# One hand-written order of 2293 steps, replaced by another order of the same steps

## The chip, the cores and the metric

The kernel runs on one core of one Trainium2 chip. The metric is the device time of one execution in microseconds (us), as the median of several runs. The core has five engines that each run their own instructions in order: TensorE (PE, matrix products; its weight loads are listed apart as PEld), VectorE (DVE), ScalarE (ACT), GpSimd (POOL) and SyncE (SP). SP here does nothing but issue DMAs. They meet only through semaphores: an instruction that needs another engine's result waits for it, and everything behind it on its own engine waits too.

## The reference

The kernel computes attention over pooled keys and values, and behind it a layer norm with a feed-forward block:

```python
def _attn_ref(q, k, v):                      # 8 batches, 8 heads, 576 rows, 64 wide
    k_p = k.reshape(B, H, S // 8, 8, D).mean(axis=3)
    v_p = v.reshape(B, H, S // 8, 8, D).mean(axis=3)
    scores = scale * np.matmul(q, k_p.transpose(0, 1, 3, 2))
    scores = scores - np.max(scores, axis=-1, keepdims=True)
    attn = np.exp(scores)
    attn = attn / (np.sum(attn, axis=-1, keepdims=True) + 1e-09)
    return np.matmul(attn, v_p)

def _moe_ref(x, g_ln, w_ch1, w_ch2):         # x: 8 x 576 x 512, w_ch1: 512 x 2048
    mu = np.mean(x, axis=-1, keepdims=True)
    var = np.mean((x - mu) ** 2, axis=-1, keepdims=True)
    xn = (x - mu) / np.sqrt(var + 1e-06) * g_ln
    ch = np.maximum(xn @ w_ch1, 0.0) @ w_ch2
    return x + ch
```

The attention's output, transposed to rows of 512, is the `x` of the second function. All is float32.

## The kernel before

The 4608 rows are 36 tiles of 128, and 9 chunks of four tiles (512 rows). Every step below is a piece of a Python generator: a call such as `A.30` (scores and softmax of tile 30) runs in several pieces, cut where the generator yields, and each piece issues a few instructions, mostly on one engine.

Attention of a tile `t`: `Q`/`A` load q (`load_q`, line 440), compute the scores on PE (line 447), on DVE the row maximum (457) and the difference `e` (460), on ACT the exponential (469) and casts to two float16 halves (480, 483), on POOL part of the second half (488, 491), and transpose through a DMA on SP (499). `B.t` multiplies with the values (534, or 536 and 537), forms the sums on DVE (544 to 554) and ACT (562) in one of 8 buffers `x`, runs the layer norm's 11 small DVE instructions (567 to 571), makes `z` on ACT (576) and from it float16 forms, which PE transposes (587) or a DMA does (613, 636). Scores and values share a pair of PSUM banks.

Keys and values of the batches are loaded and pooled: `HK` (`half_k`, line 1100) and `HV` (`half_v`, line 1103) issue one load per head or pair into a single buffer `kr` or `vr` (lines 395, 399) and fold it on DVE (1065, 1074). The last piece of `HV` runs `split_v` (line 408): a cast, and four small DMAs on ACT's own queue (lines 422, 423).

The feed-forward block keeps float32 accuracy with float16 high and low parts of weights and `z`. `R`, `C`, `M1`, `M2`, `S`, `T`, `F`, `N` load, convert, scale and split the two weight matrices, `S` with the DVE operation of line 309. Chunks 0 and 1 run it straight: `I` (`ffn_in`, matmuls of line 999), `O`/`P` (`ffn_out`, line 1034, with the sum on DVE, 1045, and the store, 1050). For chunks 2 to 8 the first product is done as seven half-size products of sums, as in Strassen's scheme: `U.c.g.n` is product `n` of group `g` of chunk `c` (`slot`, line 791; matmuls of line 726), each followed by a step that takes its bank out, on ACT (797, 801, 804) or DVE (799, 834, 851), and makes the forms in `ring` (769 to 784, 836, 845). `E.c.p.n` is the same for the second product (`slot2`, line 932; matmuls of line 943; DVE 956, 965, 975, 981, ACT 963, 967). Its weight forms come from DRAM by `D` (`w2_stream`, load of line 924) and `J`. `OUT.t` stores a finished tile from its `x` buffer (`put_out`, line 985).

What sets the order of all this is the string `START` alone (lines 56 to 200): under `tc.manual_schedule()` a loop takes its tokens from left to right, and each runs the next piece of its generator. So the order of tokens is the order of instructions on each engine and on each DMA queue (SP's, and ACT's for lines 422 and 423), and the order in which buffers and PSUM banks are taken in turn. No planner runs; there are no due times.

Of the kernel before, what the change touches and what calls it, by code (L numbers as in the profile page):

```python
# [66 lines left out]
C.2.4 I.0.0.0 A.5 I.0.0.1 I.0.0.0 C.2.2.1.1 A.5 I.0.0.0 I.0.1.0 I.0.0.1 I.0.1.0 C.2.4 I.0.0.1 S.1.4 I.0.1.0 A.5
I.0.0.0 C.2.2.1.1 R.2.7 I.0.0.0 I.0.0.1 HK.2.1 S.1.5 R.2.1 HK.2.0 A.6 I.0.1.0 S.1.5 I.0.0.1 HK.2.1 I.0.1.1
C.2.5.0.1 A.7 I.0.1.0 I.0.0.1 S.1.6 A.6 I.0.0.1 C.2.5.0.1 I.0.1.1 A.6 I.0.0.1 I.0.0.1 I.0.0.1 A.6 I.0.1.1 S.1.6
I.0.1.1 C.2.5.0.1 A.6 A.7 I.0.0.1 I.0.1.1 C.2.7 I.0.0.1 A.8 B.4 I.0.1.1 S.1.7 X.0 C.2.7 HV.2.0 I.0.1.1  # L70
C.2.5.0.1 A.6 C.2.7 HV.2.0 C.2.1.1 C.2.1.1 A.7 S.1.7 I.0.3 I.0.1.1 C.2.7 I.0.1.1 C.2.1.1 I.0.1.1 I.0.3 I.0.3
# [5 lines left out]
T.0.0.1 B.7 B.5 O.0.0 O.0.0 S.2.6 B.6 Y.2 B.6 HV.3.1 B.5 HK.2.1 T.0.0.1 HV.3.1 B.6 HK.3.0 HK.2.1 T.0.0.1 B.5
A.9 A.10 O.0.0 O.0.0 B.6 A.9 S.2.6 B.6 A.9 N.1.2 S.2.7 HV.3.1 B.6 A.9 HK.3.0 A.10 HV.3.1 O.0.0 S.2.7 A.11 A.9
HK.3.0 HK.3.0 A.10 N.1.3 O.0.1 T.1.0.1 A.9 A.10 HV.3.1 A.10 HV.3.1 T.0.1.1 HK.3.0 I.1.1 O.0.1 HK.3.1 O.0.1 B.8
T.1.0.1 I.1.3 T.0.1.1 I.1.1 B.8 HK.3.0 I.1.1 I.1.1 I.1.3 T.1.0.1 HV.3.1 I.1.3 HV.2.1 B.8 A.10 T.1.0.1 I.1.3  # L80
I.1.1 T.1.0.1 A.10 I.1.1 B.8 I.1.1 HV.2.1 T.1.0.1 HK.3.1 HV.2.1 I.1.3 HK.3.1 HK.3.1 I.1.3 I.1.3 I.1.1 B.8 I.1.1
# [1166 lines left out]
```

## Time and profile before

| what | value |
|---|---|
| median of 3 runs | 838.24 us (837.81 to 839.14) |
| profiled execution | 839.05 us |
| its span, first to last instruction | 837.3 us |
| instructions | 16786 |
| busy: PE, DVE, ACT, POOL | 799.1, 650.9, 462.5, 294.6 us |
| mean granted TensorE clock | 0.980 of full speed |
| DMA moved | 128.49 MB, mean 153 GB/s |

The page and the views come from one execution. The time outside its span, 1.75 us, is start and end of the launch. PE's busy time includes waits inside pipelined matmuls, so a share of 95% is not 95% of peak. In a view of waits, a row names the engine and operation that stood still and the instruction whose end released it. In a timeline, the text in brackets says how long the engine was idle before a row and what it had waited for; an engine with "q" behind its name is the engine's own issuing of DMAs.

### The profile page before, as it was taken

What the parts mean: (1) busy time and instruction counts of PE and PEld (TensorE: products, weight loads), DVE (VectorE), ACT (ScalarE), POOL (GpSimd) and SP (SyncE); (2) the same over time, 40 slices, a digit from 0 to 9 for tenths busy, and PEclk for the clock granted to TensorE, in tenths of its full rate; (3) what the DMA queues carried; (4) which work ended last, traced back from release to release, by engine and by line L of the source; (5) the groups of instructions that cost most, each with busy time, mean ns of one, the idle gap of its engine ahead of it and who ended that gap; (6) DMA issues with size and microseconds to landing.
All of it is one profiled execution on the core that took longest, in us unless ns stands there. A gap on an engine that the chain in (4) does not pass through costs nothing.

```text
span 837.3 us, 16786 instructions
## 1 busy us (share of the span) xinstructions
PE 799.1 (95%) x6554; PEld 624.8 (75%) x6554; DVE 650.9 (78%) x1371; ACT 462.5 (55%) x890; POOL 294.6 (35%) x260
## 2 busy tenths in 40 slices
...
GB/s 307 387 213 179 253 274 245 160 108 134 93 136 97 103 97 207 178 198 114 127 177 161 169 155 185 102 159 132 205 81 101 117 166 72 112 72 108 102 51 101
DMA packets 204639, 128.49 MB, mean 153 GB/s; under 512 B 123040, under 2 KB 181392, under 8 KB 201488
## 3 DMA queue, kind: packets, MB, share of 16 engines
...
## 4 chain that ended last, share of the span: by engine, by line
PE 63%; DVE 25%; ACT 5%; issue 3%; DMA 3%; POOL 0%; DVEq 0%; SPq 0%; ACTq 0%; POOLq 0%
PE ps_f L726 21%; PE ps_f L943 17%; PE ps_f L1034 12%; PE ps_f L999 7%; PE ps L447 2%; DVE a L516 2%; DVE x L956 2%; DVE w L309 2%; DVE y L519 2%; DVE st L567 2%; DMA pt<-phl 2%; DVE ring L784 1%; PE ps_f L1136 1%; DVE vp L1074 1%; DVE w L347 1%
## 5 line engine op out<-in xcount | busy, mean ns | idle before, releaser
L943 PE MATMUL ps_f<-w,ring 128*128 128x256 f16 x2016 | 229.0, 273 | 2.4 <-DVE ring L771 0.7
L943 PEld LDWEIGHTS <-ring 128*128 128x128 f16 x2016 | 196.3, 98 | 27.5 <-issue 2.0
L726 PE MATMUL ps_f<-zz,w 128*128 128x256 f16 x1344 | 159.6, 272 | 6.0 <-ACT v L804 5.5
L726 PEld LDWEIGHTS <-w 128*128 128x128 f16 x1344 | 130.7, 98 | 23.4 <-issue 7.2
L1034 PE MATMUL ps_f<-w,ring 128*128 128x512 f16 x576 | 127.6, 379 | 0.0
L726 PE MATMUL ps_f<-zz,raw 128*128 128x256 f16 x1008 | 120.8, 273 | 4.3 <-DVE v L834 1.8
L726 PEld LDWEIGHTS <-raw 128*128 128x128 f16 x1008 | 97.8, 98 | 18.3 <-issue 5.2
L778 POOL TENSOR_TENSOR ring<-v,ring 128x512 f16<-128x512 f32 x48 | 59.8, 1248 | 134.1 <-ACT ring L775 131.2
L1034 PEld LDWEIGHTS <-ring 128*128 128x128 f16 x576 | 56.0, 98 | 64.0 <-issue 0.2
L999 PE MATMUL ps_f<-zz,w 128*128 128x512 f16 (+1 forms) x480 | 86.9, 341 | 0.6 <-DVE ring L1013 0.5
L488 POOL TENSOR_TENSOR phl<-e,phl 128x512 f16<-128x512 f32 x31 | 37.7, 1217 | 106.8 <-ACT phl L480 85.5
L999 PEld LDWEIGHTS <-w 128*128 128x128 f16 x480 | 47.4, 100 | 36.6 <-issue 0.7
L634 POOL TENSOR_TENSOR hl<-z,hl 128x512 f16<-128x512 f32 x28 | 34.2, 1241 | 58.1 <-ACT hl L632 47.7
L447 PE MATMUL ps<-kblk,q 128*128 128x144 f32 (+1 forms) x320 | 46.3, 310 | 5.8 <-DVE e L460 3.9
L576 ACT ACTIVATE z<-x,nb,y 128x512 f32<-128x512 f32 x36 | 29.3, 815 | 40.5 <-DVE nb L571 40.5
L447 PEld LDWEIGHTS ps<-kblk,q 128*128 128x128 f32 (+1 forms) x320 | 40.5, 193 | 9.2 <-issue 5.5
L562 ACT ACTIVATE x<-ps,rs 128x64 f32<-128x64 f32 x144 | 33.0, 318 | 19.7 <-DVE x L554 15.2
L778 POOL TENSOR_TENSOR ring<-ring 128x512 f16<-128x512 f32 x24 | 29.5, 1228 | 39.8 <-ACT ring L775 36.9
L480 ACT CAST phl<-e 128x1024 f16<-128x1024 f32 x31 | 32.4, 1045 | 19.9 <-DMA pt<-phl 19.1
L469 ACT ACTIVATE e<-e 128x576 f32<-128x576 f32 x36 | 24.6, 683 | 26.0 <-DVE e L460 19.0
L1074 DVE TENSOR_REDUCE vp<-vr 72x64 f32<-72x512 f32 x48 | 32.3, 673 | 6.5 <-DMA vr<-in_v_dram 6.5
L457 DVE TENSOR_REDUCE mx<-ps 128x8 f32<-128x576 f32 x36 | 26.9, 749 | 12.0 <-PE ps L447 10.6
...
## 6 DMA issues: line engine op xcount, KB each, us to landing
...
```

What stands on the lines that cost most here:

```text
L447: nc.tensor.matmul(ps[r, p // 2, p % 2 * 2 * KV : (p % 2 + 1) * 2 * KV], lhsT=q[:, p, r], rhs=kblk[b % NKB][:, p, :], start=True, stop=True,)
L480: nc.scalar.copy(out=ph[:, :, :, 0:KA], in_=e[:, :, 0:KA].unsqueeze(1).broadcast_to([P, 2, H, KA]))
L488: nc.gpsimd.tensor_tensor(out=ph[:, 0, :, KA:P], in0=e[:, :, 0:KA], in1=ph[:, 0, :, 0:KA], op=ALU.subtract)
L562: nc.scalar.activation(out=xh[:, 4 + i, :], in_=px[:, 1, i, 0:D], func=AF.Copy, scale=rs[:, 4 + i : 5 + i])
L576: nc.scalar.activation(out=z, in_=x, func=AF.Identity, scale=y, bias=nb)
L634: nc.gpsimd.tensor_tensor(out=hl[:, 1, r], in0=part, in1=hl[:, 0, r], op=ALU.subtract)
L726: nc.tensor.matmul(ps[:, j], lhsT=w_form(wb, int(m == 2), k)[:, fs], rhs=z_form(za, int(m == 1), k), start=(first and i == 0 and j == 0), ...
L778: eng.tensor_tensor(out=lo, in0=src, in1=hi, op=ALU.subtract)
L943: nc.tensor.matmul(ps[:, i * HC : (i + 1) * HC], lhsT=h[:, hp, f, i * P : (i + 1) * P], rhs=w[:, f // FPB, wp, f % FPB], start=(first and ...
L999: nc.tensor.matmul(ps, lhsT=w[:, part, fs], rhs=zT[:, kz, cols], start=(n == 0), stop=(n == 3 * NKT - 1),)
L1034: nc.tensor.matmul(ps, lhsT=h[:, part, i, cols], rhs=w[:, wp, j], start=(n == 0), stop=(n == 3 * NFT // 2 - 1),)
L1074: nc.vector.tensor_reduce(out=vp[b][:, h, 0:D], in_=vraw.pop((b, h)), axis=AX.X, op=ALU.add,)
```

## The change

The diff has one hunk, and it is the text of `START`. Both lists hold the same 2293 tokens, each as often. 213 of them stand at the same place in the list; the mean move is 5.4 places, the longest 120. Functions, tiles, buffer counts and instructions stay. In the cut below, each group shows lines of the old list (with `-`) and the lines of the new one that stand nearest to the same steps.

```diff
...
-B.3 S.1.3 C.2.3 B.2 M1.1 A.4 C.2.3 A.4 I.0.0.0 B.3 C.2.0.1.1 C.2.0.1.1 C.2.3 B.3 C.2.4 C.2.0.1.1 I.0.1.0
-I.0.0.0 B.3 C.2.0.1.1 M1.1 B.2 I.0.1.0 R.2.2 C.2.3 A.4 A.5 B.2 R.2.5 A.4 I.0.0.0 I.0.1.0 A.6 I.0.0.0 M1.1 B.3
+S.1.3 A.4 C.2.3 S.1.3 C.2.3 I.0.1.0 M1.1 B.2 A.4 C.2.0.1.1 C.2.0.1.1 HK.2.0 C.2.4 B.3 I.0.0.0 M1.1 B.3 C.2.3
+C.2.0.1.1 B.3 M1.1 C.2.0.1.1 I.0.0.0 I.0.0.0 R.2.2 I.0.1.0 B.2 B.2 B.2 A.5 A.5 A.4 C.2.3 B.3 S.1.4 I.0.1.0
...
-C.2.1.1 I.0.3 A.7 I.0.1.1 M2 Y.0 A.7 I.0.1.1 B.4 X.1 T.0.0.1 M2 I.0.2 M2 T.0.0.1 HV.2.0 HK.2.0 I.0.3 HV.2.0
-S.2.0 I.0.3 I.0.3 HK.2.1 A.7 B.4 S.2.0 HK.2.0 I.0.2 T.0.0.1 A.8 I.0.3 B.4 N.0.0 S.2.1 B.5 A.9 A.7 T.0.0.1 Y.1
-I.0.3 I.0.3 T.0.0.1 B.4 HV.2.0 I.0.3 B.4 I.0.2 HV.2.0 I.0.2 B.4 I.0.3 T.0.0.1 B.4 X.3 A.8 S.2.1 I.0.2 T.0.0.1
-I.0.2 I.0.2 S.2.2 A.8 B.5 I.0.2 B.7 A.8 S.2.2 HV.2.0 A.8 S.2.3 I.0.2 I.0.2 HV.3.1 B.7 I.0.2 A.8 B.7 S.2.3 O.0.0
+I.0.1.1 I.0.1.1 I.0.3 A.7 T.0.0.1 I.0.1.1 M2 I.0.3 I.0.1.1 HK.2.0 M2 M2 B.5 X.1 A.7 I.0.3 HV.2.0 T.0.0.1 B.4
+I.0.2 T.0.0.1 A.7 S.2.0 I.0.3 S.2.0 B.4 I.0.2 HK.2.0 HV.2.0 T.0.0.1 T.0.0.1 B.4 HK.2.1 A.7 I.0.3 I.0.3 A.8 A.8
+Y.1 HV.2.0 B.4 I.0.3 I.0.3 HV.2.0 S.2.1 I.0.3 I.0.2 I.0.2 B.4 I.0.2 B.4 I.0.3 X.3 A.8 A.8 N.0.0 I.0.2 B.4 A.9
+S.2.1 T.0.0.1 S.2.2 T.0.0.1 I.0.2 N.0.1 I.0.2 B.5 A.8 B.7 HV.2.0 S.2.2 S.2.3 I.0.2 B.7 B.7 Y.3 S.2.3 I.0.2
...
-E.3.1.6 U.4.0.2 D.3.1.3 U.3.3.4 B.19 E.3.1.2 A.21 U.3.3.3 HV.5.1 E.3.1.5 E.3.1.6 HV.5.1 A.21 U.4.0.2 A.21
-E.3.1.6 A.22 E.3.1.5 U.4.1.1 E.3.1.3 A.21 A.22 A.22 HV.5.1 A.22 HV.5.1 U.4.0.6 E.3.1.3 U.4.1.6 U.4.0.6 OUT.14
-D.3.1.2 U.4.1.2 U.4.1.6 HK.6.0 HV.5.1 A.23 A.22 U.4.0.6 B.21 HV.5.1 U.4.1.6 U.4.0.7 U.4.1.2 A.22 B.21 U.4.1.7
+U.3.3.7 U.3.3.4 B.19 B.19 D.3.1.2 B.19 A.21 B.19 U.4.1.1 B.19 U.4.0.1 B.19 B.19 U.4.0.2 U.3.3.3 U.3.3.3 U.3.3.4
+U.3.3.4 E.3.1.2 E.3.1.2 E.3.1.6 U.3.3.4 U.3.3.4 HV.5.1 U.3.3.3 U.3.3.3 U.3.3.4 U.3.3.4 E.3.1.5 HV.5.1 A.21
+U.4.0.2 U.4.0.2 A.22 E.3.1.5 E.3.1.3 HK.6.0 U.3.3.7 E.3.1.6 E.3.1.6 A.21 A.21 U.4.1.1 HV.5.1 HK.6.0 HV.5.1 A.22
+A.22 E.3.1.3 U.4.1.6 A.22 U.4.0.6 U.4.1.2 A.23 U.4.1.6 A.22 U.4.1.6 U.4.0.6 U.4.0.6 OUT.14 HV.5.1 B.21 U.4.1.7
+B.21 U.4.0.7 U.4.1.2 U.4.1.2 B.21 A.22 HV.5.1 U.4.0.5 U.4.0.5 B.21 E.3.1.7 U.4.0.7 U.4.0.7 HK.6.1 U.4.0.7
...
-B.21 U.4.1.2 B.21 U.4.0.5 E.3.1.7 U.4.0.5 U.4.0.7 B.21 HK.6.0 U.4.0.7 U.4.0.4 D.4.0.0 E.3.1.7 HK.6.1 HK.6.0
-U.4.0.7 E.3.1.4 U.4.0.4 E.3.1.4 U.4.0.4 U.4.1.5 D.4.0.1 U.4.0.4 U.4.0.4 OUT.15 U.4.0.4 U.4.0.4 E.4.0.1 OUT.13
-U.4.1.5 U.4.0.4 HK.6.1 U.4.1.7 HK.6.0 HK.6.1 U.4.1.7 U.4.0.3 D.4.0.2 E.4.0.1 U.4.1.7 OUT.12 U.4.1.4 U.4.0.3
+U.4.2.1 E.4.0.5 E.4.0.3 OUT.13 U.4.2.1 B.20 U.4.2.2 B.21 B.21 B.21 D.4.1.0 U.4.2.6 A.24 E.4.0.3 B.21 B.21
+HV.6.1 A.25 U.4.2.6 U.4.2.5 A.24 B.21 HV.6.1 U.4.2.2 U.4.2.7 E.4.0.7 U.4.2.5 U.4.2.7 U.4.2.2 U.4.2.7 B.23 A.24
+A.24 B.23 B.23 HV.6.1 U.4.2.3 U.4.2.3 HV.6.1 OUT.12 E.4.1.1 U.4.2.3 B.22 B.23 U.4.2.4 U.4.2.4 E.4.1.1 U.4.3.6
...
-B.20 HV.6.1 U.4.2.2 E.4.0.7 A.24 HV.6.1 B.23 U.4.2.7 U.4.2.5 U.4.2.2 U.4.2.3 B.23 B.23 U.4.2.7 A.24 E.4.1.1
-HV.6.1 U.4.2.7 U.4.2.3 HV.6.1 B.23 U.4.2.3 U.4.2.7 U.4.2.4 D.4.1.2 E.4.1.1 U.4.3.6 U.4.2.4 B.23 E.4.0.4 HV.6.1
+HV.6.1 A.25 U.4.2.6 U.4.2.5 A.24 B.21 HV.6.1 U.4.2.2 U.4.2.7 E.4.0.7 U.4.2.5 U.4.2.7 U.4.2.2 U.4.2.7 B.23 A.24
+A.24 B.23 B.23 HV.6.1 U.4.2.3 U.4.2.3 HV.6.1 OUT.12 E.4.1.1 U.4.2.3 B.22 B.23 U.4.2.4 U.4.2.4 E.4.1.1 U.4.3.6
...
-HV.6.0 B.22 B.23 A.25 B.23 B.23 E.4.1.3 D.5.0.0 E.4.1.7 A.25 B.23 HV.6.0 B.23 HV.6.1 U.5.0.1 B.23 E.4.1.3 A.25
-B.23 HV.6.1 E.4.1.4 U.5.0.1 HV.6.1 OUT.18 HV.6.1 E.4.1.4 OUT.17 A.25 U.5.1.1 HV.6.1 HV.6.1 B.24 U.5.0.2 U.5.1.1
+HV.6.0 E.4.1.2 B.23 E.4.1.5 E.4.1.5 B.22 B.23 B.23 B.23 B.23 B.23 B.23 A.25 E.4.1.7 D.5.0.0 E.4.1.3 A.25 HV.6.0
+E.4.1.7 E.4.1.4 HV.6.1 HV.6.1 HV.6.1 B.23 E.4.1.3 OUT.16 E.4.1.4 OUT.19 OUT.17 HV.6.1 U.5.0.1 U.5.0.1 U.5.1.1
...
-E.5.1.7 B.27 HV.7.0 B.27 B.27 A.29 HV.7.0 A.30 B.27 B.27 A.29 U.6.1.2 D.6.0.0 B.27 E.5.1.7 A.29 B.27 E.5.1.4
-HV.7.0 A.29 U.6.1.2 HV.7.1 E.5.1.4 A.29 HV.7.1 E.5.1.3 D.6.0.1 HV.7.1 HV.7.1 U.6.1.2 OUT.23 OUT.21 HV.7.1
-HV.7.1 A.30 E.6.0.1 E.5.1.3 A.30 U.6.0.5 OUT.20 U.6.0.6 A.30 U.6.0.5 OUT.22 U.6.0.3 U.6.0.6 D.6.0.2 E.6.0.1
-U.6.1.6 U.6.0.6 U.6.0.3 U.6.0.3 U.6.0.7 U.6.1.6 U.6.1.6 U.6.1.5 U.6.0.7 U.6.0.7 U.6.0.4 U.6.0.7 U.6.1.7 U.6.0.4
+HV.7.0 B.27 E.5.1.5 U.6.1.1 A.29 A.30 E.5.1.7 B.27 B.27 B.27 D.6.0.0 B.27 U.6.1.2 A.29 A.29 E.5.1.7 E.5.1.4
+B.27 U.6.0.2 HV.7.0 E.5.1.4 A.29 A.29 OUT.21 U.6.1.2 E.5.1.3 HV.7.1 HV.7.1 U.6.0.2 U.6.1.2 HV.7.1 HV.7.1 HV.7.1
+HV.7.1 E.6.0.1 D.6.0.2 U.6.0.5 U.6.0.5 U.6.0.6 A.30 E.5.1.3 A.30 U.6.0.3 U.6.0.6 U.6.0.3 U.6.0.6 U.6.1.6
+U.6.0.3 U.6.0.7 U.6.1.6 U.6.1.6 U.6.0.7 U.6.1.5 U.6.0.4 D.6.0.1 OUT.23 E.6.0.1 U.6.0.7 U.6.0.7 U.6.1.7 U.6.0.4
...
-B.29 U.6.2.4 B.30 U.6.3.2 B.28 U.6.2.3 U.6.3.7 U.6.2.7 A.32 U.6.2.7 U.6.3.2 B.30 E.6.1.1 U.6.2.4 B.30 U.6.2.3
-U.6.2.4 U.6.3.5 D.6.1.2 E.6.1.1 B.30 U.6.3.5 U.6.2.4 U.6.2.3 U.6.3.3 U.6.3.7 U.6.2.4 U.6.2.3 U.6.2.4 U.6.2.4
-U.6.3.4 U.6.3.7 U.6.2.4 U.6.3.3 B.29 B.31 U.6.3.3 U.6.3.7 B.31 U.7.1.1 U.6.3.4 U.7.0.1 U.6.3.3 U.6.3.4 E.6.1.2
+B.29 B.29 U.6.3.5 U.6.3.6 U.6.3.7 B.30 B.29 U.6.3.2 D.6.1.0 U.6.2.7 A.32 U.6.3.2 B.30 U.6.2.7 B.30 B.31 B.31
+U.6.2.3 E.6.1.1 U.6.2.4 U.6.3.5 U.6.3.3 U.6.2.4 U.6.2.3 U.6.2.4 B.30 U.6.2.3 U.6.3.7 E.6.1.1 U.6.3.4 U.6.2.3
+U.6.2.4 U.6.2.4 U.6.2.4 U.6.2.4 U.7.0.1 U.6.3.3 D.6.1.2 B.29 U.6.3.7 U.6.3.3 U.7.1.1 U.6.3.4 U.6.3.4 U.6.3.3
...
-B.34 U.7.2.3 B.34 A.35 B.33 U.7.2.7 U.7.2.4 D.7.1.1 B.34 B.33 U.7.2.7 U.7.3.1 B.33 B.33 E.7.0.3 U.7.3.1 B.33
-B.33 U.7.2.4 B.33 U.7.3.2 E.7.0.4 U.7.2.4 U.7.2.4 U.7.2.4 B.35 B.32 U.7.3.2 U.7.2.4 U.7.3.5 B.35 B.34 U.7.3.6
-U.7.3.2 U.7.2.3 E.7.1.1 E.7.0.3 U.7.2.4 B.34 U.7.3.6 B.35 D.7.1.2 E.7.1.1 B.35 U.7.2.4 B.34 U.7.3.5 U.7.3.6
-U.7.3.3 U.7.2.3 U.7.2.3 U.7.3.7 U.7.3.3 B.35 U.7.3.7 U.7.3.3 B.35 U.7.3.7 U.7.3.4 B.35 U.8.0.1 U.7.3.7 B.33
+E.7.0.4 A.35 U.7.2.7 U.7.3.1 U.7.2.4 B.33 E.7.0.3 U.7.2.7 B.33 OUT.25 B.33 U.7.2.7 B.34 U.7.3.1 B.33 U.7.2.4
+U.7.3.2 B.32 U.7.3.5 U.7.2.3 E.7.0.4 B.33 E.7.0.3 B.35 U.7.2.4 B.33 U.7.2.4 U.7.2.4 U.7.2.4 U.7.3.2 U.7.3.5
+U.7.2.4 B.35 B.35 U.7.3.2 B.34 B.34 U.7.2.3 U.7.2.3 U.7.3.6 U.7.2.3 U.7.3.6 E.7.1.1 E.7.1.1 U.7.3.6 D.7.1.1
+B.35 U.7.3.3 U.7.3.7 B.35 B.34 U.7.3.7 U.7.3.7 U.7.3.4 B.33 B.33 D.7.1.2 U.8.0.1 U.7.3.3 U.7.3.3 U.8.0.1 B.35
...
```

Of the moves that the prediction speaks of: in the groups in turn, `M1.1`, `A.4` and `I.0.0.0`; `A.8`, `S.2.1`, `I.0.2` and `B.4`; `HV.5.1`, `A.22`, `E.3.1.3` and `D.3.1.3`; `OUT.12` and `OUT.13`; `B.22`, `B.23` and `A.25`; `E.4.1.4` and `HV.6.1`; `HV.7.1`, `A.30`, `U.6.0.5`, `D.6.0.1` and `OUT.23`; `U.6.3.5`; and `U.7.3.5` with `B.35`.

## Rows read from the trace of the kernel before

**Rows 1.** The page's engine totals: busy us, share of the span, instructions.
```profile
PE 799.1 (95%) x6554; PEld 624.8 (75%) x6554; DVE 650.9 (78%) x1371; ACT 462.5 (55%) x890; POOL 294.6 (35%) x260
```
**Rows 2.** The page's chain that ended last, by engine.
```profile
PE 63%; DVE 25%; ACT 5%; issue 3%; DMA 3%; POOL 0%; DVEq 0%; SPq 0%; ACTq 0%; POOLq 0%
```
**Rows 3.** Windows: stretch, length, busy us by engine, granted clock, DMA share, GB/s.
```profile
40.00:60.00 20.00, 15.58 (x73) 10.61 (x72) 19.17 (x44) 17.98 (x25) 1.02 (x1) 0.67 0.57 211
160.00:360.00 200.00, 199.93 (x1330) 120.90 (x1329) 146.65 (x310) 90.32 (x183) 86.28 (x70) 1.00 0.50 127
600.00:602.00 2.00, 2.00 (x21) 1.78 (x20) 0.92 (x3) 0.00 (x0) 0.00 (x0) 1.00 1.09 192
602.00:604.00 2.00, 1.89 (x18) 1.54 (x16) 0.07 (x1) 0.00 (x0) 0.00 (x0) 1.00 1.10 287
600.00:620.00 20.00, 16.68 (x157) 14.30 (x156) 9.57 (x17) 9.62 (x17) 4.63 (x5) 1.00 0.48 136
720.00:740.00 20.00, 18.50 (x193) 16.56 (x191) 18.91 (x47) 12.78 (x29) 9.05 (x9) 1.00 0.50 120
```
**Rows 4.** Waits of PE: us in total, times, longest.
```profile
PE ps_f L726 <- ACT v L804: 5.5, 3, 3.2
PE ps L447 <- DVE e L460: 3.9, 1, 3.9
...
PE ps_f L726 <- DVE v L834: 1.8, 2, 1.5
PE ps_f L726 <- DVE v L981: 1.6, 2, 1.3
PE ps L536 <- DVE sm L544: 1.4, 1, 1.4
...
PE ps L447 <- ACT x L562: 0.7, 1, 0.7
...
PE ps_f L587 <- ACT z L576: 0.6, 1, 0.6
...
PE ps_f L943 <- ACT ps_f L967: 0.5, 1, 0.5
```
**Rows 5.** Timeline of ACT, 596 to 609: start, length, instruction, idle before.
```profile
599.94 0.52 ACTq L422 DMA_DIRECT2D va<-vh  x1
603.92 0.68 ACTq L423 DMA_DIRECT2D vb<-vh  x1
604.64 0.68 ACT L469 ACTIVATE e<-e 128x576 f32<-128x576 f32 x1 [6.65 <-DVE w L799]
...
606.51 0.58 ACT L804 COPY v<-ps_f 128x512 f32<-128x512 f32 x1
```
**Rows 6.** Timeline of all engines, 117.9 to 122.
```profile
117.97 3.22 DVE L309 SCALAR_TENSOR_TENSOR w<-w,ws 128x1024 f16<-128x1024 f32 x1
117.98 2.13 POOL L676 TENSOR_TENSOR w<-w 128x1024 f32<-128x1024 f32 x1
...
121.72 0.74 DVE L460 TENSOR_TENSOR e<-ps,mx 128x576 f32<-128x576 f32 x1
```
**Rows 7.** Timeline of all engines, 421.5 to 427.
```profile
422.01 0.50 SPq L399 DMA_DIRECT2D vr<-in_v_dram  x1
...
426.69 0.68 DVE L1074 TENSOR_REDUCE vp<-vr 72x64 f32<-72x512 f32 x1 [2.38 <-DMA vr<-in_v_dram]
```
**Rows 8.** Waits of DVE for transfers: us in total, times, longest.
```profile
DVE vp L1074 <- DMA vr<-in_v_dram: 6.5, 4, 2.4
...
DVE x L554 <- DMA out_dram<-x: 4.2, 1, 4.2
```
**Rows 9.** Line 499's issues on SP: ns min/median/max, first and last start.
```profile
L499 SPq DMA_TRANSPOSE pt<-phl x31: 1347/2356/5191, 85.4 to 721.7; - x31
```
**Rows 10.** Line 309's splits of the second weights: the same columns, shape.
```profile
L309 DVE SCALAR_TENSOR_TENSOR w<-w,ws x8: 1273/1418/3250, 109.7 to 150.7; 128x1024 f16<-128x1024 f32 x8
```

More of the change, by code (lines that the diff above doesn't have):

```diff
@@ L67 @@
[L67 to L71, printed above, removed]
@@ L77 @@
[L77 to L81, printed above, removed]
@@ new lines @@
+U.5.0.4 U.5.0.4 HK.7.0 U.5.0.4 HK.7.0 U.5.0.3 A.26 A.26 U.5.2.6 U.5.1.6 A.26 OUT.18 U.5.0.3 U.5.1.7 U.5.1.7
+A.27 B.24 U.5.1.7 U.5.1.3 U.5.0.4 HK.7.0 U.5.1.4 U.5.1.3 U.5.1.4 U.5.1.3 HK.7.1 U.5.2.1 U.5.1.4 B.25 U.5.3.1
+E.5.0.2 A.26 A.26 HK.7.0 U.5.1.4 U.5.1.4 U.5.1.4 U.5.1.4 U.5.1.4 A.27 E.5.0.2 U.5.2.1 U.5.1.3 U.5.2.6 U.5.1.3
+HV.7.1 U.5.2.2 A.28 HV.7.1 HV.7.1 HK.7.1 A.27 E.5.0.6 B.25 U.5.2.6 HK.7.1 U.5.2.7 B.26 U.5.2.2 D.5.0.3 A.27
+A.27 U.5.2.2 E.5.0.5 E.5.0.6 A.27 U.5.3.1 HK.7.1 E.5.0.6 B.26 E.5.0.7 D.5.1.0 HV.7.1 HV.7.1 B.25 B.25 E.5.0.5
@@ new lines @@
+E.6.1.2 D.6.1.3 U.6.3.4 B.31 U.7.0.1 U.6.3.3 U.7.0.2 U.6.3.3 U.6.3.4 U.6.3.7 E.6.1.2 U.6.3.4 E.6.1.6 U.6.3.4
+B.31 U.6.3.4 U.7.0.2 E.6.1.6 E.6.1.6 B.31 B.31 E.6.1.5 E.6.1.5 B.31 B.31 B.31 B.31 B.31 B.31 U.7.0.2 A.32 A.32
+E.6.1.7 D.7.0.0 E.6.1.3 A.32 U.7.1.1 E.6.1.7 E.6.1.4 E.6.1.4 U.7.1.2 U.7.1.2 E.6.1.3 A.32 A.32 A.33 A.33 A.33
+U.7.0.5 U.7.0.6 U.7.0.5 A.33 OUT.24 A.33 D.7.0.1 A.33 U.7.1.6 A.33 U.7.0.6 U.7.1.2 U.7.0.3 U.7.1.6 U.7.0.3
+U.7.0.6 U.7.0.7 OUT.27 U.7.0.7 U.7.1.6 U.7.1.7 U.7.0.7 U.7.0.7 U.7.0.4 U.7.0.3 U.7.1.5 U.7.0.4 U.7.1.5 U.7.1.7
```

212 lines of the change are left out of this document (106 added, 106 removed).

## The prediction

> **What bounds the kernel now.** I read five views, from the coarse to the fine. The engine totals [rows 1] first: TensorE (PE) is busy 799.1 of 837.3 us; VectorE (DVE) comes second with 650.9. The chain of the work that ended last agrees [rows 2]: 63% of it is PE, 25% DVE, 3% each issue and DMA. An order that only shuffles work behind PE cannot win; it wins where PE stands.
>
> The windows say where that is [rows 3]. From 160 to 360 us PE is busy 199.93 of 200: nothing is to be had there unless a new wait is made. From 40 to 60 us it is the other way round: PE 15.58, DVE 19.17 of 20, the mean granted TensorE clock 0.67 of full speed; DVE carries the start. From 600 to 620 us PE has 16.68 with DVE at only 9.57, so that gap is a matter of order and not of work; from 720 to 740 PE has 18.50 and DVE 18.91, so that one is not.
>
> The waits of PE [rows 4] give the prices, and short timelines the places.
>
> The profiled execution took 839.05 us (837.3 of span and 1.75 around it), 0.81 above the median of the runs, 838.24. The sum is made against the first and its result taken off the second.
>
> **The change part by part.** The list holds the same 2293 steps, so instruction counts, tiles and bytes stay, and a step's own durations are those of the trace. Counted in the two lists, off the longest common order are 58 of PE's 456 steps, 156 of DVE's 672, 172 of ScalarE's (ACT) 619, 35 of POOL's 208 and 95 of the SP queue's 311. What is left is which wait ends sooner and which later.
>
> *The gap at 604 us.* PE's longest wait there, 3.2 us, is for a copy of ACT, line 804 [rows 4]. ACT's own rows tell why [rows 5]: the last step of HV.7.1 issues four small DMAs on ACT's queue, the third at 599.94 for 0.52 us, the fourth only at 603.92. That is 3.46 us in which ACT's queue is held, by what the view does not say; the transfers were dense then, DMA share 1.09 and 1.10 from 600 to 604 [rows 3], and I take it for an issue that waited until an earlier DMA had landed. Behind it come the exponential of A.30 (604.64) with its casts, and only then the copy that PE needs (606.51, 0.58 long). In the new list that copy (second step of U.6.0.5) stands ahead of A.30's exponential, and two DMAs of SP that stood just ahead (D.6.0.1, OUT.23) come after. If the hold goes, the copy no longer bounds PE: −3.2. If the hold ends at 604.60 as before, the copy ends at about 605.2 instead of 607.1: −1.9. I take −3.0. Late next is A.30's exponential, for which no matmul waits in this stretch.
>
> *Waits of PE that a nearer neighbour fills.* (a) The 0.6 us for z, line 576 [rows 4]: a step of the first matmul (I.0.2) moves ahead of the transposes that wait: −0.6, bounds 0 and −0.6. (b) The 1.4 us at line 536: two DVE steps of A.8 (the one in the rows takes 0.74 us) now stand ahead of a split that took 3.22 [rows 6], so the bank comes free some 3 to 4 us sooner: −1.2, bounds 0 and −1.4. (c) The waits for ACT x (0.7) and ACT ps_f (0.5) [rows 4]: in the one another tile's values take the bank's turn, in the other a product step moves ahead of the pooled maximum: −1.0, bounds 0 and −1.2. (d) Line 804 is waited for twice more, 5.5 − 3.2 = 2.3 us together [rows 4]: some 0.7 at 658 us and 1.5 at 737. At 658 the product whose copy is waited for stands three PE steps sooner: −0.7, bounds 0 and −0.7. (e) At 737, and at 741 for DVE v, line 834 (1.5) [rows 4], U.7.3.5 moves ahead and its copy with it; but DVE is full there [rows 3], and one of the two releases is DVE's: −0.9 of 3.0, bounds 0 and −3.0.
>
> Sum of the gains: 3.0 + 0.6 + 1.2 + 1.0 + 0.7 + 0.9 = 7.4, from 1.9 (only the copy's place) to 10.1.
>
> *Steps that come later.* (f) In the start, the DVE work ahead of the first matmul of line 999 grows by a step like that of rows 6 (0.74 us) and shrinks by about 0.5, and a maximum of the weights of like length moves ahead of steps that feed PE. DVE has no slack there [rows 3], so it counts in full: +0.8, bounds −1.5 and +2.5 (three such steps more, two less). PE's 3.9 us for DVE e, line 460 [rows 4], lies in this stretch and stays, for one more conversion stands ahead of its releaser.
> (g) At 426 us PE waits 1.3 of the 1.6 us of DVE v, line 981 [rows 4]. That step stood behind a fold of V, which waited 2.38 us for its load [rows 7]. The new list puts A.22's score maximum and e (one like rows 6, 0.74, each) behind this fold and ahead of line 981: if the load lands as before, PE's wait grows by 1.5; if it lands sooner, since the stream load ahead of it on SP is now another one that waits less for PE, by nothing: +0.5, bounds 0 and +1.5. The vr buffer is single, so a load starts only when the previous fold has read it, and landed 4.68 us after its issue here (422.01 to 426.69 [rows 7]). Between some folds the new list leaves less DVE work than the old: HV.5.0's from 3.5 to 1.6 us, HK.3.0's from 3.8 to 1.9, and six more of HV by 0.5 to 1.9; elsewhere more. DVE now waits 6.5 us in all for vr, in 4 of 48 folds [rows 8]. I count +0.5, bounds −1.0 and +3.3 (half of those 6.5 again).
> (h) Result stores move back: OUT.12, 13, 18 and 25 by 59 to 118 places, some of them past transposing DMAs, each of which holds SP for 1.35 to 5.19 us, median 2.36 [rows 9]. The x buffers number 8; a later store frees its buffer later, and the sums of a coming tile wait. The trace has one such wait, 4.2 us, line 554 [rows 8]. Set beside the trace's times, most moved stores have 4 to 7 us between issue and reuse, so 0 to 2 to spare if a store lands like that load of 4.68: I take +1.2, half a median transposing DMA, for one that misses; bounds 0 and +4.2.
>
> Sum of the losses: 0.8 + 0.5 + 0.5 + 1.2 = 3.0, from −2.5 to +11.5.
>
> Net −4.4: 839.05 − 4.4 = 834.65 for the profiled execution, 838.24 − 4.4 = 833.8 for the median.
>
> **A rule weighed.** The split at 117.97 us took 3.22 [rows 6], where the shortest of its kind took 1.273 and the median one 1.418 [rows 10]: something held it for about 1.9 us, and an addition of POOL ran beside it from 117.98 to 120.11 [rows 6]. The Trainium skill, "SBUF — State Buffer", section "Who interferes with whom", says that VectorE and GpSimd share a pair of SBUF ports under an exclusive lock, and that a VectorE instruction with two SBUF inputs is blocked for the whole of a GpSimd one that reads SBUF. By that rule, the trace agrees here: 2.13 us of POOL and then 1.1 of DVE. It speaks against the change, since steps moved singly get new partners by chance; what it gives is the fourth rival.
>
> **The rivals.**
> *DVE takes back what the order gives.* PE's gains bring nothing where DVE is the next to end: from 720 to 740 us, and in the start [rows 3]. For it: a quarter of the chain is DVE already [rows 2]. Against it: from 600 to 620 us DVE is half idle. If only the copy's place at 604 (−1.9) and (a) (−0.6) count, against (f), (g) and half of (h), 0.8 + 1.0 + 0.6 = 2.4, the time is 838.24 − 0.1 = 838.1.
> *Slower: late stores and loads.* SP works its queue in order and so does DVE, so a store or a vr load behind a held step makes DVE wait and PE after it. It decides from two stores that each miss by a median transposing DMA, 2 × 2.36 [rows 9], with vr at its upper bound, 3.3: with (f) and the fold at 426 that is 4.7 + 3.3 + 0.8 + 0.5 = 9.3 of losses, against gains of 6 (a late x also spoils (e) and part of (c)): +3.3, 841.5. For it: the spare times of 0 to 2 us, and rows 8. Against it: only one store and four vr loads were waited for so far.
> *The hold at 604 us stays, the rest as forecast*: 3.0 − 1.9 = 1.1 less gained, 834.9; it lies inside the forecast's own range.
> *POOL and DVE meet otherwise.* If two more of the splits in the DVE-bound start meet POOL in full, 2 × (3.25 − 1.27) = +4.0 [rows 10]: 837.8; two less, 829.8.
>
> **How the numbers follow.** Forecast 0.57, with the hold as before in it (831 to 836.5, all faster); DVE takes it back 0.17 (836.6 to 839.8, no change); late stores and loads 0.20 (840 to 844, slower); other meetings of POOL and DVE 0.06, half faster, the rest one third no change and two thirds slower. What a measurement of this kernel can tell from no change is 0.2%, 1.7 us: 836.6 to 839.9. So faster 0.60, same 0.18, slower 0.22. The range leaves out about 0.1 on either side: 827.5, where the gains go to their upper bound and the losses to nearly nothing, and 841.
>
> **What would show it.** Right: no wait of PE above 1 us between 596 and 612; the copy of line 804 ahead of A.30's exponential on ACT; line 726's wait for ACT v down from 5.5 to below 2.5; the waits of (a) to (c) gone from PE's list. Wrong: DVE's waits of line 554 on stores and of line 1074 on vr above 16 us together (10.7 now); the first matmul of line 999 over 2 us later; PE below 199 of 200 from 160 to 360 us. If PE's busy time itself, 799.1, moves by over 2 us, the clock or the pace changed and the sum misses the cause.

## The result: 1.7% faster, 10 us more than forecast

The new list takes 824.35 us (median of 4 runs, 823.53 to 824.70) where the old one took 838.69 beside it: a ratio of 0.983 (new time by old), 95% interval 0.981 to 0.984, 14.3 us less. Below, the numbers in brackets behind a time are this ratio to the old list run beside it, and its interval. I had forecast 833.8, and the lower end of my range was 827.5. The direction was right, the size was not. The profiled execution of the new list took 823.53 us, with a span of 821.8.

The page of the new list: its engine totals, and the chain that ended last, by engine.
```profile
PE 794.1 (97%) x6554; PEld 623.8 (76%) x6554; DVE 645.3 (79%) x1371; ACT 461.2 (56%) x890; POOL 289.8 (35%) x260
...
PE 84%; DVE 10%; DMA 2%; ACT 1%; issue 1%; POOL 1%; ACTq 0%; SPq 0%; DVEq 0%; POOLq 0%
```
PE's share of the chain went from 63% [rows 2] to 84%, DVE's from 25% to 10%: the new list is a list in which PE seldom waits. Its windows, columns as in [rows 3]; 580 to 600 is the stretch that lay at 592 to 612 before:
```profile
40.00:60.00 20.00, 13.65 (x68) 9.09 (x70) 19.36 (x45) 18.28 (x26) 0.00 (x0) 0.84 0.62 227
...
160.00:360.00 200.00, 200.00 (x1351) 122.20 (x1350) 151.37 (x317) 89.11 (x178) 85.30 (x71) 1.00 0.51 126
...
580.00:600.00 20.00, 19.37 (x178) 17.21 (x177) 12.48 (x28) 10.98 (x20) 3.64 (x5) 1.00 0.99 214
```
The DVE-bound start is as it was, 160 to 360 us stayed full, and the hole of 3.3 us at 604 [rows 3] is down to 0.6. The waits of PE in the new list, columns as in [rows 4]:
```profile
PE ps L447 <- issue: 5.2, 1, 5.2
PE ps L534 <- ACT pt L478: 1.8, 2, 1.1
PE ps_f L999 <- DVE allmax L302: 1.6, 1, 1.6
PE ps_f L943 <- DVE ring L771: 1.5, 2, 1.2
PE ps_f L726 <- ACT ps_f L801: 0.9, 1, 0.9
PE ps_f L726 <- DVE v L834: 0.9, 1, 0.9
...
PE ps_f L943 <- DVE v L851: 0.9, 1, 0.9
PE ps_f L726 <- ACT v L804: 0.6, 1, 0.6
PE ps_f L943 <- DMA w<-d2B: 0.6, 1, 0.6
```
Line 804 fell from 5.5 us [rows 4] to 0.6, and the waits that I had called (a), (b) and (c) are gone. The cost of a wait can be worked out from the starts of successive matmuls (start to start, less the usual pace of that form): behind the first 75 us the old list has 30 waits that cost some 0.2 us or more each, 22.2 in all, the new one 12 that cost 7.7. The idle time that the profile prints for the 30 is 17.2 us; each costs some 0.17 more than is printed, since the overlap of the matmul before it is lost too (in the rows at 607 us below, twelve matmuls are printed with 1.47 us and the next begins 1.31 behind their start). 22.2 − 7.7 = 14.5, near the 14.8 that the table below has for this pair of profiles between 90 us and the end. (The new list's first wait of line 999, 1.6 us, begins just ahead of 75 us and is not among the 12. The two spans differ by 15.5 us.)

Where the offset arises shows when I ask at what time PE has done the same amount of matmul work as the old list's profile had (us against that profile; one execution each):

| list | 90 | 160 | 345 | 460 | 590 | 620 | end |
|---|---|---|---|---|---|---|---|
| old, again | +0.6 | +0.2 | +0.2 | −1.0 | −1.3 | +0.6 | +0.5 |
| new | −0.7 | −4.1 | −4.8 | −8.4 | −10.8 | −13.6 | −15.5 |
| new, again | +0.5 | −2.9 | −3.6 | −5.8 | −8.1 | −11.7 | −14.3 |
| new in the first third only | −0.4 | −3.8 | −4.0 | −5.6 | −4.9 | −3.2 | −3.4 |
| new in the middle only | +0.2 | +0.2 | −0.5 | −2.8 | −5.2 | −6.0 | −5.6 |
| new in the last third only | +0.3 | −0.1 | −0.2 | −1.6 | −1.9 | −5.3 | −8.4 |

### The profile page after: what moved, and what is told of

Its sections match the earlier page's. It is cut to its first block, busy times and chain, and to the rows that moved or that the text cites. A ratio compares the mean times of both kernels' runs of the same rounds, so it can differ in the third digit from the quotient of the medians.

```text
span 821.8 us, 16780 instructions
## 1 busy us (share of the span) xinstructions
PE 794.1 (97%) x6554; PEld 623.8 (76%) x6554; DVE 645.3 (79%) x1371; ACT 461.2 (56%) x890; POOL 289.8 (35%) x260
## 4 chain that ended last, share of the span: by engine, by line
PE 84%; DVE 10%; DMA 2%; ACT 1%; issue 1%; POOL 1%; ACTq 0%; SPq 0%; DVEq 0%; POOLq 0%
PE ps_f L726 27%; PE ps_f L943 23%; PE ps_f L1034 15%; PE ps_f L999 10%; PE ps L447 4%; PE ps_f L1136 1%; PE ps L536 1%; PE ps L537 1%; DMA pt<-phl 1%; DVE w L347 1%; PE ps L534 1%; PE ps_f L1152 1%; DMA w<-in_kn_dram 1%; DVE x L956 1%; DVE a L516 1%
## 5 line engine op out<-in xcount | busy, mean ns | idle before, releaser
L778 POOL TENSOR_TENSOR ring<-v,ring 128x512 f16<-128x512 f32 x48 | 57.5, 1201 | 158.3 <-ACT ring L775 142.7
L775 ACT CAST ring<-v 128x512 f16<-128x512 f32 x48 | 29.7, 618 | 9.6 <-DVE v L784 5.8
L1011 ACT ACTIVATE ring<-ps_f 128x512 f16<-128x512 f32 (+1 forms) x40 | 19.7, 509 | 27.0 <-PE ps_f L999 18.2
```

What stands on the lines that cost most here:

```text
L775: nc.scalar.copy(out=hi, in_=src)
L778: eng.tensor_tensor(out=lo, in0=src, in1=hi, op=ALU.subtract)
```

## Experiments

**Three stretches, each alone in the new order.**
```diff
-START = old[0:656] + old[656:1668] + old[1668:]
+START = in_new_order(old[0:656]) + old[656:1668] + old[1668:]
...
+START = old[0:656] + in_new_order(old[656:1668]) + old[1668:]
...
+START = old[0:656] + old[656:1668] + in_new_order(old[1668:])
```


> Old list, but its first 656 steps (up to the product U.2.1.5, 240 us in the trace of before) stand in the new order. Theory A (each wait of PE goes because of the steps that stand next to it, so the stretches are independent and their gains add up): -4.6 us against before, the offset that the new kernel's trace has at that place, kept to the end: about 834.0. Theory B (one cause, the order of the transfers or a luckier start, lets everything behind it run smoother): more than half of the whole -14.3, so below 831.5.

> Old list, but steps 657 to 1668 (240 to 590 us in the trace of before) stand in the new order, the start and the end as before. Theory A: the offset grows only in this stretch, by 11.3 - 4.6 = 6.7 us: about 832.0. Theory B: without the new start next to nothing of it, above 836.

> Old list, but the steps from 1669 on (590 us to the end) stand in the new order. Theory A: -3.7 to -4.2 us (15.5 - 11.3, of which 2.6 at the 604 us gap): about 834.7. Theory B: above 837.


Measured: 835.71 (0.997, interval 0.996 to 0.998), 831.81 (0.993, 0.991 to 0.995) and 830.5 (0.991, 0.990 to 0.993), beside 837.81: −2.1, −6.0 and −7.3, in sum −15.4 of −14.3. So there is no single cause: each stretch brings its own gain, as theory A says. Of its three sizes only the middle one came out. The first stretch brought 2.1 of 4.6 us: its profile is 4 us ahead until 460 us and loses again at 504 to 506 us (two waits, 0.35 and 0.86) and at 604 us. The last one brought 7.3 where 3.7 to 4.2 were expected, a figure from one pair of profiles; by the table, the two lists run again lie 6.8 us apart at 590 us and 14.8 at the end, 8.0 us from there on. PE's rows behind the gap at 604 us show why one pair of profiles is not enough. First those of the old list's first profile, then those of its second, with the second's window of 608 to 610 (columns as in [rows 3]):
```profile
607.13 1.47 PE L726 MATMUL ps_f<-zz,w 128*128 128x256 f16 x12 [3.25 <-ACT v L804]
608.44 1.47 PE L726 MATMUL ps_f<-zz,raw 128*128 128x256 f16 x12
```
```profile
606.00 2.20 PE L726 MATMUL ps_f<-zz,w 128*128 128x256 f16 x12 [3.50 <-ACT v L804]
607.99 2.46 PE L726 MATMUL ps_f<-zz,raw 128*128 128x256 f16 x12
...
608.00:610.00 2.00, 2.00 (x11) 1.45 (x10) 0.69 (x1) 0.63 (x1) 0.00 (x0) 0.50 0.43 155
```
After PE had stood for 3.50 us the granted clock fell to 0.50, the lower of its two levels (1.2 instead of 2.4 GHz), and the 24 matmuls behind it took 4.28 us from start to start instead of 2.62: 1.7 us more. The clock fell the same way behind this wait in the list with only the first third new (3.28 us) and in that with the late stores (3.79), but not behind the 3.25 us of the first profile, and in no profile of the new list. So the gap at 604 us cost the old list 3.4 us in one execution and 5.3 in another.

**The transfers by themselves.**
```diff
-all 2293 steps as in the old list
+steps that only issue a transfer on SP: in the new list's order; all others: as in the old list
...
+steps that only issue a transfer on SP: in the old list's order; all others: as in the new list
```


> The steps that only issue a transfer on SP (311 of 2293: loads, stores, transposes through a DMA) stand among themselves nearly as in the new list, all steps with arithmetic exactly as in the old one. Theory A (the places of arithmetic steps remove PE's waits): at most -2 us, 837 to 839, or slower if a load comes late. Theory B (the order of the transfers): most of the gain, below 830. The long wait of PE at 604 us goes under B and stays or shortens to some 2 us under A.

> The counterpart: all arithmetic steps exactly as in the new list, the steps that only issue a transfer on SP among themselves nearly as in the old one. Theory A: nearly all of the gain stays, 824.5 to 827. Theory B: most of it is gone, above 832.


Measured: 851.76 (1.017, 1.015 to 1.019), 13.9 us slower than the old list, and 833.84 (0.994, 0.992 to 0.996), which keeps 4.8 of the 14.3 us. Neither theory had this: the order of transfers alone is a loss, the order of the arithmetic without them gives up two thirds. (Some 30 steps could not be exchanged without breaking a dependence, so the split is not quite clean.) The waits of PE with the new transfers under the old arithmetic show the price:
```profile
PE ps_f L943 <- DMA w<-d2T: 4.8, 2, 4.3
PE ps_f L943 <- DMA w<-d2B: 4.8, 2, 2.7
```
9.6 us for weight loads that come late, a wait that the profile of the old list does not have at all. Behind three of the four (2.75 us at 366, 4.31 at 444, 2.06 at 661) the granted clock fell to 0.50 for 3.4 us each, an estimated 1.6 us of PE each time by the 604 us rows above. With the old transfers under the new arithmetic PE waits for transposing transfers instead:
```profile
PE ps L536 <- DMA pt<-phl: 3.9, 1, 3.9
PE ps_f L726 <- DMA zz<-hl: 2.1, 1, 2.1
```
The old list's profile has 0.6 and 0.2 us of these two, the new one's none; behind the first the clock was at 0.50 from 363 to 370 us. My slower rival, late transfers, is real; the new list avoids it because it moved transfers and arithmetic together, since either order without the other brings late transfers.

**The gap at 604 us, taken apart.** Three lists, each the old one but for the steps shown (the first has moves at 114, 121 and 426 us too, told below; the second exchanges D.3.1.2 and D.3.1.3; the third moves V.1's small transfers in the start):
```diff
-A.30 U.6.0.5 OUT.20 U.6.0.6 A.30 U.6.0.5
+U.6.0.5 U.6.0.5 A.30 OUT.20 U.6.0.6 A.30
...
-A.29 HV.7.1 E.5.1.3 D.6.0.1 HV.7.1 HV.7.1 U.6.1.2 OUT.23 OUT.21 ... U.6.0.4
+A.29 HV.7.1 E.5.1.3 HV.7.1 HV.7.1 U.6.1.2 OUT.21 ... U.6.0.4 D.6.0.1 OUT.23
...
-HV.7.1 A.30 E.6.0.1 E.5.1.3 A.30 ... U.6.0.6
+A.30 E.6.0.1 E.5.1.3 A.30 ... U.6.0.6 HV.7.1
```


> Old list with six steps moved by hand, at four places, arithmetic only: U.6.0.5's matmuls and copy ahead of A.30's exponential (604 us); A.8's e ahead of the split S.2.1 (121 us); two pieces of I.0.2 ahead of B.4's transposes (114 us); the fold of HV.5.1 ahead of A.22's maximum and e (426 us). Theory A: PE's waits at 114 and 121 us go (-0.8 and -1.5), the one at 604 shrinks to 1.3 or less (-2 to -3.4), and at 426 the wait of 1.34 grows by up to 1.5, as I predicted. Sum -3 to -5.7: 833 to 835.7. If the hold of ACT's queue decides at 604 us and not the copy's place, that wait stays above 2.

> Old list with only transfers moved at the same places: the stream load D.6.0.1 and the store OUT.23 behind U.6.0.4 (604 us), and the loads D.3.1.3 and D.3.1.2 exchanged (426 us). If the long issue of ACT at 600.5 to 603.9 us comes from dense transfers on SP, it shortens and PE's wait of 3.25 falls by what it shortens. If the wait for vr at 426 us came from D.3.1.3 standing in front of it on SP, the fold starts earlier and PE's 1.34 goes. Theory A expects neither by more than half: 836.5 to 838.7.

> Old list with only the two steps moved that issue the four small transfers on ACT's own queue: HV.7.1's last step behind the copies that PE waits for at 604 us, and V.1's behind A.3's probability cast in the start. If the held queue of ACT is the cause at 604 us, PE's wait of 3.25 us there goes whole (-3.4) with nothing else changed, and the held issue, if it still comes, makes no one wait. If the hold was only put down to ACT, the wait stays. In the start: -0.5 to -3 if ACT's issues delay A.3's chain, nothing if DVE bounds it.


PE's wait there, 3.25 before, was 1.51, 1.94 and 1.85 us, with the clock at 1.00 behind it; the times, beside 838.63, were 837.98 (0.999, 0.997 to 1.001), 836.49 (0.998, 0.996 to 0.999) and 834.09 (0.994, 0.992 to 0.997). ACT's timelines tell why none took it whole. With the copy moved ahead:
```profile
598.19 0.49 ACTq L422 DMA_DIRECT2D va<-vh  x1
602.36 0.68 ACTq L423 DMA_DIRECT2D vb<-vh  x1
603.08 0.58 ACT L804 COPY v<-ps_f 128x512 f32<-128x512 f32 x1 [6.77 <-DMA va<-vh]
```
The hold is still there, 598.68 to 602.36, and the copy comes right behind it. With the two SP transfers moved away instead:
```profile
596.58 0.68 ACTq L423 DMA_DIRECT2D vb<-vh  x1
597.30 0.68 ACT L469 ACTIVATE e<-e 128x576 f32<-128x576 f32 x1 [3.30 <-DVE x L956]
600.06 1.04 ACT L480 CAST phl<-e 128x1024 f16<-128x1024 f32 x1 [2.08 <-DMA pt<-phl]
...
601.21 0.58 ACT L804 COPY v<-ps_f 128x512 f32<-128x512 f32 x1
```
The hold is gone, but A.30's cast now waits 2.08 us for A.29's transposing transfer, which still reads the cast's buffer, and the copy stands behind that. The third list shows the same, a cast that waited 3.80 us. Its 4.5 us are more than the 1.4 gained at this wait; up to 1.7 more can be the clock that did not fall, and where the rest came from, its one profile does not tell (V.1's move shows no gain that can be told in the start: 0.3 us at 90 us). The first list gained 1.7 us at this wait, but its time is the same as before within the interval. So two waits stood in series, and taking one away uncovered the other. Both moves together:

> Old list with four steps moved, all at 604 us: U.6.0.5's matmuls and copy ahead of A.30's exponential, and D.6.0.1 and OUT.23 behind U.6.0.4. Theory: the wait there had two causes in series, ACT's queue held by its fourth small transfer (ends with A.29's transposing transfer), and behind it A.30's cast that waits for the same transfer. Either move alone left 1.5 and 1.9 us; both together leave 0.3 or less: -3.4 us, 834.5 to 835.5. If one of the two was chance, the wait stays above 1.


Measured: 834.34 against 838.53 (0.995, 0.993 to 0.997), −4.2; PE has no wait there at all. ACT:
```profile
597.87 0.67 ACTq L423 DMA_DIRECT2D vb<-vh  x1
600.00 0.59 ACT L804 COPY v<-ps_f 128x512 f32<-128x512 f32 x1 [4.62 <-PE ps_f L726]
600.48 0.69 ACT L469 ACTIVATE e<-e 128x576 f32<-128x576 f32 x1
```
ACT now waits for PE. Four moved steps give 4.2 us (interval 2.8 to 5.9) of the 14.3 that the whole new list gives; that it is more than the wait's own 3.4 fits a clock that no longer falls, but lies within the interval. That the hold ends with the landing of A.29's transfer itself is argued from its place, not shown by a row, and the two transfers ahead of it are not the whole cause: in the list with only the middle new they stand as in the old list, yet the fourth small transfer went out right behind the third (596.08 and 596.60), and PE waited 0.7 us there.

**At 114, 121 and 426 us**, the other moves of the first of these lists: I.0.2's pieces, A.8's e and HV.5.1's fold. Inconclusive in the first two places: PE's waits at 114 and 121 us (2.0 together) belong to some executions only. In this one, as in four others with the old steps there, a wait of 1.3 us stands at 106 us instead, in three of the others with one of 0.3 to 0.6 at 142; here 0.4 and 1.3 (for a transposing transfer) came at 122 and 131 us besides, so nothing was gained. At 426, PE waited 0.2 us though the fold waited 3.8 for vr; I had expected 1.34 and up to 1.5 more. (The exchange of D.3.1.2 and D.3.1.3 in the second list tells nothing about this wait, which the next runs show to be one execution's.)

**The old and the new list once more.**


> The old list once more, unchanged. If PE's wait of 1.34 us at 426 us belongs to the list, it is there again with 1.3. If it belonged to that one execution (a transposing transfer on SP that took 5.0 us to issue), it is gone or below 0.3, as in three other kernels whose steps at that place were the old ones. The waits at 604 (3.25), 736 and 740 (1.50, 1.52) are there to 0.1 under every theory. Time 837 to 839.

> The new list once more, unchanged, as the mate of the next kernel. Time 823 to 826; the waits of 0.86 (377 us), 1.16 (485) and 0.91 (726) come back to 0.1; those that end with a transfer (0.62 at 640 us) need not.


839.0 and 823.92 us (0.982, 0.981 to 0.984). In the old list PE's wait for DVE v, line 981, was 0.2 us and no longer 1.6 [rows 4]. SP's timeline in the first profile of the old list, then in the second:
```profile
416.93 5.00 SPq L636 DMA_TRANSPOSE zz<-hl  x1
422.01 0.50 SPq L399 DMA_DIRECT2D vr<-in_v_dram  x1
```
```profile
417.17 4.17 SPq L636 DMA_TRANSPOSE zz<-hl  x1
421.43 0.50 SPq L399 DMA_DIRECT2D vr<-in_v_dram  x1
```
In the first profile one transposing transfer took 0.83 us longer to issue, and the load of vr behind it went out 0.58 us later. It also took longer to land: the fold that needs it began 4.68 us after the issue there [rows 7], and 3.03 in the second profile, at 424.46. Why, the rows don't tell; 1.3 us of PE followed. It happened in one of the seven profiles in which the steps at that place are old. The waits of 1.50 and 1.52 at 736 and 740 us, which arithmetic sets, came back to 0.03 in every list that has the old steps there; the one at 604 us did not, 3.25 and then 3.50. In the new list 0.86 at 377 us, 1.16 at 485 and 0.91 at 726 came back to 0.1, the 0.63 at 593 did not come back, and a new one of 0.94 stood at 363.

**The late stores alone.**
```diff
-... OUT.13 ... OUT.12 ... OUT.18 ... OUT.25
+the same four tokens 65 to 119 places later
```


> Old list with only the four result stores OUT.12, 13, 18 and 25 moved to where the new list has them, 65 to 119 places later. As I predicted (h): a coming tile waits for its x buffer, +1.2 us, up to +4.2, seen as DVE waits of line 554 on a store beyond the 4.2 us that the old list has at its start. Theory now: these stores have slack, no new wait of line 554, PE's waits from 436 us on as before to 0.1, 838 to 839.


Measured: 840.8 against 837.67 (1.004, 1.002 to 1.005), 3.1 us slower. DVE has one wait for a store more than before, 1.07 us at 516 us, so the theory that these stores have slack falls for DVE. DVE's waits for stores there, and a wait of PE at 510 us (0.4 before):
```profile
DVE x L554 <- DMA out_dram<-x: 5.7, 2, 4.6
```
```profile
PE ps_f L293 <- DVE rowmax L271: 1.3, 1, 1.3
```
But PE's wait ends at 510 us, ahead of DVE's, and from there to 580 us PE has no other: the store's wait reaches PE nowhere in these rows. Ahead of PE's wait a DVE step that began just behind a POOL step was stretched, first in this list, then in the old one; that it set PE's wait is argued from its place:
```profile
504.26 1.16 POOL L634 TENSOR_TENSOR hl<-z,hl 128x512 f16<-128x512 f32 x1 [1.60 <-issue]
504.40 1.30 DVE L627 TENSOR_TENSOR z<-z 128x256 f32<-128x256 f32 x1
```
```profile
505.94 0.42 DVE L627 TENSOR_TENSOR z<-z 128x256 f32<-128x256 f32 x1
```
The list with only the first third new has the same stretched step (1.30), PE's wait (0.86) and a wait of line 554 (1.28 us), with these stores in their old place. At 604 us PE waited 3.79 with the clock at 0.50 behind it, but the old list's second profile has nearly as much. So the 3.1 us are measured; that the late stores cost them by way of the x buffers, as (h) has it, is not shown. In the new list line 554 waits for no store.

**Waits that are left in the new list.**
```diff
-... V.1 ... A.3  C.1.6 A.3  B.3 M1.1  B.17 ... U.3.2.3  U.4.3.4 A.25 U.4.3.3  HV.7.1 ... U.6.0.6  U.7.3.4 ... U.8.0.1
+... A.3 V.1  A.3 C.1.6  M1.1 B.3  U.3.2.3 B.17  U.4.3.3 U.4.3.4 A.25  ... U.6.0.6 HV.7.1  U.8.0.1 U.7.3.4
```


> The new list with seven steps moved by hand at PE's waits that are left in it: V.1's four small transfers on ACT behind A.3's probability cast; the maximum M1.1 ahead of B.3's layer norm and A.3's e ahead of C.1.6 (start); U.3.2.3's bank ahead of B.17's forms (377 us); U.4.3.3's forms ahead of U.4.3.4's (485); HV.7.1's small transfers behind U.6.0.6 (592); U.8.0.1 ahead of U.7.3.4 (726). Theory (each wait goes by its neighbours): -0.8 to -1 each at 377, 592 and 726, -1 at 485 unless the later form is then late, -0.7 to -2 in the start: 820 to 822. Rival (the list is balanced as a whole, a wait removed comes back a little later): 823.5 to 825.


Measured: 825.04 (0.984, 0.982 to 0.987), no gain. (The exchange at 485 us lets one form of U.4.3.3 read a sum before U.4.3.4 has renewed it: other values, the same instructions.) The waits at 377 and 592 us went; the 1.16 at 485 came back as three, 1.6 in sum:
```profile
PE ps_f L943 <- DVE ring L778: 0.9, 2, 0.6
PE ps_f L943 <- ACT ring L775: 0.7, 1, 0.7
```
and 0.91 at 726 became 1.29. In the start nothing was gained that can be told: by the reckoning of the table the profile stands at −1.2 us at 90, the new list's three between −1.6 and +0.5. Then only the two moves that had worked, beside the new list:
```diff
-... B.17 ... U.3.2.3 ... HV.7.1 E.6.0.1 ... U.6.0.6
+... U.3.2.3 B.17 ... E.6.0.1 ... U.6.0.6 HV.7.1
```


> The new list with the two of the seven moves that took their wait away without another one behind it: U.3.2.3's bank ahead of B.17's forms (377 us, -1.0) and HV.7.1's small transfers on ACT behind U.6.0.6 (592 us, -0.8, or 0 in an execution where that wait is absent anyway). Theory: 822 to 823.5, 1 to 1.8 below the new list. Rival (a wait removed comes back later): the same as the new list within 0.5.

> The new list unchanged, as the mate of the kernel before on the same chip: 823.5 to 824.5.


823.37 (0.983, 0.981 to 0.986) and 823.14 (0.982, 0.980 to 0.985): the waits at 377 and 592 are gone, some 1.8 us by their cost, but 5 runs each, which scatter over 2 to 4 us, don't show it. No version beats the new list by more than can be told.

## Why the prediction was wrong

The mechanism held: PE's waits end sooner because other steps stand next to them, 160 to 360 us stayed full, and the named waits went. What failed is the sum. Its step "Sum of the gains: 7.4, from 1.9 to 10.1" was too small: by cost 14.5 us went behind the start, over its upper bound, because it priced only the waits that I had named, (e) among them too low, and put the many small ones at nothing without a reason. And of the step "Sum of the losses: 3.0" nothing that can be told arrived.

- *604 us*: −3.0 forecast; the wait cost 3.41 and 3.66 us in two profiles of the old list, 0.79 and nothing in two of the new: −2.6 to −3.7. Right for the wait, though I saw only one of the two causes: A.30's cast would have held the copy even without the hold. The 1.7 us at the lower clock behind it, in the second of the two, was in no term of mine.
- *(a) and (b)*: −1.8 forecast, −2.3 by cost; from 100 to 350 us PE has no wait left that the profile prints. But the two moves alone did not do it, and in about half of the executions with the old steps the waits themselves stood elsewhere. The fourth rival also came in its good direction, which I gave 0.03. Line 309's splits in the new list, columns as in [rows 10]:
```profile
L309 DVE SCALAR_TENSOR_TENSOR w<-w,ws x8: 1271/1276/1278, 109.0 to 144.6; 128x1024 f16<-128x1024 f32 x8
```
None of them is stretched any more, where the longest was 3.25 us and the median 1.418; DVE has that much less to do in a stretch where it was nearly full. In both profiles of the old list the longest took 3.2, in both of the new 1.28. The rule of the Trainium skill ("SBUF — State Buffer", "Who interferes with whom") says more than I drew from it: the port pair that the two engines share is an exclusive lock, and the order of issue decides which of them is blocked. The traces agree that either one can be: in [rows 6] the split paid, 3.22 us beside 2.13 of POOL; in the list with moves at 114, 121, 426 and 604 us such a split took its plain 1.27, and POOL paid:
```profile
138.51 1.27 DVE L309 SCALAR_TENSOR_TENSOR w<-w,ws 128x1024 f16<-128x1024 f32 x1
138.54 3.24 POOL L676 TENSOR_TENSOR w<-w 128x1024 f32<-128x1024 f32 x1
```
That the order of issue decides, these rows don't show, since the split begins 0.01 us ahead of POOL in the one and 0.03 in the other; the DVE step at 504 us above, which began 0.14 us behind POOL and took 1.30 instead of 0.42, agrees. In that list the longest split took 1.75 us, and yet PE's waits between 100 and 150 us cost 3.5 there and 3.1 in the old list's first profile. So shorter splits alone do not take PE's waits away; whether they have a share in the new list's 2.3 us stays open.
- *(c), (d), (e)*: −2.6 forecast; 1.5, 0.9 and 2.3 by cost, 4.7. The term (e) was sized down to 0.9 because DVE is full from 720 to 740; it was order there too.
- *Waits that I did not list*: 21 of the old list's 30, 0.2 to 0.8 us each, cost 9.2 us; the new list has ten others that cost 5.8, four of them 0.8 to 1.3. Net −3.4, forecast 0. This is the largest miss of any one term.
- *(f)*: +0.8 forecast; at 90 us the profiles of the new list stand 0.7 and 1.6 before and 0.5 behind the first of the old one, and the second of the old 0.6 behind it: no loss that can be told. The clock in 40 to 60 us was 0.67 in one profile of the new list and 0.84 in the other, so a start cannot be weighed from one execution. My sign for a cause that the sum misses came up here: PE's busy time fell by 5.0 us, 799.1 to 794.1, with a mean granted clock of 0.980 and then 0.985. In the second pair (0.980 and 0.978) it fell by 2.3, 799.2 to 796.9. Part of it is the waits themselves, an estimated 18 × 0.17 = 3.1 us that the profile counts as busy around the 18 waits that went; the rest of the 5.0 fits the higher clock of that start.
- *(g)*: +1.0 forecast. DVE's waits for vr did rise, 6.5 [rows 8] to 8.6 us, but the waits of PE show no loss from it; and the 1.34 us at 426 that I built on was one execution's, so 0 to −1.5. I had also overlooked that DVE's waits for kr, not among the [rows 8], were larger than those for vr, so "only one store and four vr loads" was wrong. The old list, then the new:
```profile
DVE zs L1065 <- DMA kr<-in_kT_dram: 7.5, 4, 4.6
```
```profile
DVE vp L1074 <- DMA vr<-in_v_dram: 8.6, 8, 2.5
DVE zs L1065 <- DMA kr<-in_kT_dram: 1.2, 1, 1.2
```
Stores, kr and vr together fell from 18.2 to 9.8 us.
- *(h)*: +1.2 forecast, 0 seen. When the stores move alone the time rises by 3.1 us, but through no store that the rows show. The error of the losses to learn from is plainest in the transfers by themselves: I priced each moved transfer against the old neighbours, but its user had moved too. Under the old arithmetic the new transfers cost 13.9 us, together with their users none that can be told. Losses of single moves cannot be added up where the list moves both sides.

Sum for the first pair of profiles, behind the start: −2.6 − 2.3 − 4.7 − 3.4 − 1.5 (426 us) = −14.5, against a forecast of −7.4 + 2.2. Of the 9.3 us between the two, 7.1 are gains that I left out or sized too low, 2.2 are losses that did not come. That the 1.5 us at 426 are among the gains is luck of the first profile.
